# Half of the query transfers of a gated-attention kernel's first blocks issued from GpSimd and ScalarE

## The chip, the core and the metric

The kernel runs on one core of a Trainium2 chip. The metric is the time of one execution on the device in microseconds (us); the kernel before takes 1825.69 us, the median of three runs (1825.0 to 1826.87).

## What is computed

A linear attention whose state is a complex matrix that decays at each step, followed by a mixture of experts whose gates are balanced by eight rounds of normalizing rows and columns. Cut to what matters:

```python
# attention: B, H, S, D = 4, 8, 768, 48; a = a_re + i*a_im, scaled to magnitude <= 0.999
for t in range(S):
    S_ = a[t][:, None] * S_ + outer(k[t], v[t])      # S_ is complex, D x D for each head
    y[t] = q[t] @ real(S_)
x = y as [B*S, H*D]                                  # 3072 x 384
P = sinkhorn(exp(x @ w_gate), 8 rounds)              # 3072 x 8
out = sum over e of P[:, e] * (relu(x @ w1[e]) @ w2[e])
```

## The kernel before

**Blocks.** The 3072 positions are cut into 12 blocks of 256, three for each batch entry, and a block into two halves of 128 (`c` = 0, 1). Phase 1 goes through the blocks. For block i the elementwise part (`elem` and `chain`) normalizes the decays, forms their running products z (complex, two planes `a` = 0, 1 for real and imaginary) with a scan on VectorE (lines 304 to 309), and writes keys divided by the product into `kh` (line 416) and queries times the product back into `z` (line 418), channels on the partitions. Then `mix(i)` does the attention of the block in a chunked form, and two experts' layers for the block before it (`experts`, lines 164 to 193) are interleaved with it on TensorE: each step has a first layer `ph`, two evictions on ScalarE (`hh` line 191, `hf` line 192), a difference on VectorE (`hl`, line 193), and a second layer that runs three steps later (LAG = 3). Phases 2a and 2b do the remaining six experts and touch none of this.

**Transfers to head layout.** `mix` needs keys and queries with a head's channels on the partitions. For each half c it copies `kh` into `ks` and `z` into `qs` (lines 430 to 435): for each of the two tiles, both planes and three channel tiles, 12 transfers of 16 partitions by 8 heads by 128 positions (129 for `qs`; the last column is the state's decay over the half). A transfer is 64 KB, both sides in SBUF. The real plane goes to partitions 0 to 47, the imaginary one to 64 to 111. There are two buffers each of `qs` and `ks`, used by halves in turn.

**What follows.** TensorE transposes the keys (`keys`, line 454), multiplies keys by queries into scores (`scores`, line 468), and forms the state's update `U` (line 463). VectorE copies the scores under a causal mask into `sc` (line 471). `outs` (line 485) multiplies `sc` by the values and the old state by `qs`. VectorE then moves the state on (lines 511 to 522), and the output goes through ScalarE (`xh`, line 524) and VectorE (`xl`, line 525) to the experts.

**Order.** TensorE's instructions run in the order in which the program writes them. On the other engines and queues a scheduler orders them by program order and by its own estimate of when each is ready; each engine then works through its list in order, a transfer's issue among them: an issue that has to wait holds up what stands behind it. All transfers go through SP's queue, apart from two of the first `z`. In block 0 the instructions of `mix` on ScalarE and VectorE are told to stand behind the elementwise part, and the first weights are loaded in thirds (line 145) between its steps, behind the transfers on SP. `self.ql[i]` remembers a block's last transfer; the loads of `qk` (line 335) and `z` (line 333) of later blocks are told to stand behind it on SP. The blocks of `chain` that matter on ScalarE are the squares (lines 385, 391, 394, 405) and the reciprocal roots (lines 390, 410).

Of the kernel before, what the change touches and what calls it, by code (L numbers as in the profile page):

```python
# [20 lines left out]
NCH = SUB // CH  # L21
# [39 lines left out]
class Net:  # L61
# [134 lines left out]
    def phase1(self, c1, ca):  # L196
# [45 lines left out]
        for i in range(ns):  # L242
            mix = self.mix(i)
            if i == 0:
                n = 0
                while True:
                    with tc.issue_after(self.sqs[0, 1].ins), tc.issue_after(self.zl[0, 1].ins):
                        if next(mix, self) is self:
                            break
                    with tc.issue_after(self.sqs[0, 1].ins):  # L250
                        for _ in range(2 if n else 0):
                            if late and next(late[0], self) is self:
                                late.pop(0)
                                next(late[0], None) if late else None
                    n += 1
                for g in late:
                    for _ in g:
                        pass
                with tc.issue_after(self.gl.ins):
                    m = self.marks  # L260
                    self.behind = [m[j] for j in (0, 0, 0, 2, 2, 2, 3, 3, 3, 4, 5, 5)]
                    self.elem(1)
                edge = mybir.DependencyInfo(mybir.DependencyClass.NoSync, mybir.DependencyReason.DATA)
                for ins in self.casts:
                    tc.add_manual_dep(ins.ins, self.nrm.ins.name, edge, reason="casts behind the norm")
                continue
            lg = self.logits(i - 1)
            for n in range(2 * NF):
                with ExitStack() as st:
                    if i == 1 and n in (4, 5):  # L270
                        st.enter_context(tc.issue_after(self.sqs[1, n - 4].ins))
                        st.enter_context(tc.issue_after(self.zl[1, n - 4].ins))
                    self.moe.send((i - 1, n // NF, n % NF))
                if i == 1 and n == 2:
                    for ins in self.post[1]:
                        tc.add_manual_dep(ins.ins, self.hf.ins.name, edge, reason="chain behind the step")
                if n in (1, 2):
                    next(lg)
                if n >= LEAD.get(i, 4):
                    next(mix, None)  # L280
# [140 lines left out]
    def mix(self, i):  # L421
        nc, tmp = self.nc, self.tmp
# [5 lines left out]
        for c in range(NCH):  # L428
            ib = (i * NCH + c) % 2
            qs, ks, rr, rn = self.qs[ib], self.ks[ib], self.rr[ib], self.rn[ib]  # L430
            for dst, src, w in ((ks, kht, CH), (qs, zt, CH + 1)):
                for a in range(2):
                    for ct in range(NCT):
                        q = 64 * a + 16 * ct
                        dma = nc.sync.dma_start(dst[q:q + 16, :, :w], src[:, a, ct * NCH + c, :w])
            self.ql[i] = dma
            R = qs[:, :, CH]
            first = (i % self.nsub == 0) and c == 0
            lastc = (i % self.nsub == self.nsub - 1) and c == NCH - 1
# [576 lines left out]
```

## Time and profile before

| | us |
|---|---|
| median of the runs (lowest, highest) | 1825.69 (1825.0, 1826.87) |
| the profiled execution's own time | 1826.91 |
| its span, first to last instruction | 1825.0 |
| TensorE busy | 1767.9 |
| VectorE busy | 1358.4 |
| ScalarE busy | 733.1 |
| GpSimd busy | 6.4 |

Times in the rows are microseconds from the first instruction of the span, unless they say ns. PE is TensorE, PEld its weight loads, DVE VectorE, ACT ScalarE, POOL GpSimd, SP SyncE; a q behind a name (SPq, ACTq) is the engine's queue of instructions that issue transfers, wait or branch. L435 is line 435. `out<-in` are the program's names of what is written and read. In brackets at the end of a row stands how long the engine had been idle before it, and what ended that. PEclk is the share of TensorE's full clock that was granted: 1.00 is 2.4 GHz, 0.50 is 1.2 GHz.

### The profile page before, as it was taken

Reading aid. Unit: us, or ns where it says so; the run is one execution under the profiler, and the core shown is the slowest. Engines: PE = TensorE matmul, PEld = TensorE weight load, DVE = VectorE, ACT = ScalarE, POOL = GpSimd, SP = SyncE. Lnnn points to the kernel's source line nnn. Section 1 sums busy time; section 2 is a strip of 40 time slices with the busy share of each in tenths; the row PEclk is TensorE's granted clock in tenths of the full one; section 3 lists DMA queues with packets and bytes.
Section 4 is the critical chain, followed back from the end, with each engine's and each line's share of the span. In section 5 each row is a group of like instructions: output and inputs, shape, how many; then the busy total and the mean of one; then the engine's idle time right before and its main releaser. Section 6 shows DMA issues by size and latency. Waiting matters only on the chain.

```text
span 1825.0 us, 30537 instructions
## 1 busy us (share of the span) xinstructions
PE 1767.9 (97%) x12024; PEld 1726.8 (95%) x12024; DVE 1358.4 (74%) x3023; ACT 733.1 (40%) x1606; POOL 6.4 (0%) x15
## 2 busy tenths in 40 slices
PE   5899999999999999999999999999999999999998
PEld 3889899999999999899999999999999999999998
DVE  7898899889883587867576767687776767675754
ACT  7544444554543443434242424243433333342421
POOL 1000000000000000000000000000000000000000
PEclk9999999999999999999999999999999999999999
DMA  6334333433332431402020101232220101020100
GB/s 210 108 104 117 103 112 112 119 112 115 115 105 93 132 92 38 136 2 69 1 69 1 53 18 53 70 96 78 87 70 18 53 18 52 3 69 1 53 27 28
DMA packets 120632, 132.83 MB, mean 73 GB/s; under 512 B 9632, under 2 KB 100512, under 8 KB 120480
## 3 DMA queue, kind: packets, MB, share of 16 engines
q1 hardware_dynamic: 119680, 130.41, 23.3%
q8 instruction: 96, 1.57, 0.4%
q14 instruction: 56, 0.46, 0.1%
q10 hardware_dynamic: 800, 0.39, 0.1%
HBM read 88.22 MB, written 23.59 MB: 61 GB/s over the span
## 4 chain that ended last, share of the span: by engine, by line
PE 86%; DVE 8%; DMA 3%; ACT 1%; issue 1%; SPq 1%; DVEq 0%; ACTq 0%
PE po L741 10%; PE po L739 10%; PE po L740 10%; PE P L778 9%; PE P L780 9%; PE P L779 9%; PE po L164 4%; PE ph L186 3%; PE ph L187 3%; PE ph L185 3%; PE po L166 3%; PE po L165 3%; PE sp L468 3%; PE y L485 2%; PE U L463 1%
## 5 line engine op out<-in xcount | busy, mean ns | idle before, releaser
L741 PE MATMUL po<-wc,hl 128*128 128x384 f32 x1152 | 385.7, 335 | 2.9 <-DVE hl L800 2.9
L739 PE MATMUL po<-wc,hh 128*128 128x384 f32 x1152 | 385.2, 334 | 0.4 <-ACT hh L799 0.4
L740 PE MATMUL po<-wc,hh 128*128 128x384 f32 x1152 | 385.2, 334 | 0.0
L799 ACT ACTIVATE hh<-c 128x384 fp32r<-128x384 f32 x384 | 200.9, 524 | 322.1 <-DVE c L788 320.7
L800 DVE SCALAR_TENSOR_TENSOR hl<-c,hh 128x384 fp32r<-128x384 f32 x384 | 211.8, 552 | 65.8 <-ACT hh L799 58.0
L741 PEld LDWEIGHTS po<-wc,hl 128*128 128x128 f32 x1152 | 216.5, 188 | 4.4 <-DVE hl L800 4.4
L739 PEld LDWEIGHTS po<-wc,hh 128*128 128x128 f32 x1152 | 216.5, 188 | 0.7 <-ACT hh L799 0.7
L740 PEld LDWEIGHTS po<-wc,hh 128*128 128x128 f32 x1152 | 216.4, 188 | 0.0
L793 ACT ACTIVATE s<-P 128x384 f32<-128x384 f32 x192 | 94.1, 490 | 275.0 <-PE P L780 275.0
L191 ACT ACTIVATE hh<-ph 128x256 fp32r<-128x256 f32 x192 | 73.1, 381 | 249.4 <-PE ph L187 248.9
L186 PE MATMUL ph<-xl,w 128*128 128x256 f32 x576 | 162.9, 283 | 2.8 <-DVE xl L525 2.8
L185 PE MATMUL ph<-xh,w 128*128 128x256 f32 x576 | 162.2, 282 | 0.6 <-ACT xh L524 0.6
L187 PE MATMUL ph<-xh,w 128*128 128x256 f32 x576 | 162.5, 282 | 0.0
L778 PE MATMUL P<-B,wa 128*128 128x384 f32 x480 | 160.4, 334 | 0.6 <-DVE c L788 0.6
L780 PE MATMUL P<-B,wa 128*128 128x384 f32 x480 | 160.4, 334 | 0.0
L779 PE MATMUL P<-B,wa 128*128 128x384 f32 x480 | 160.3, 334 | 0.0
L164 PE MATMUL po<-w,hh 128*128 128x384 f32 x384 | 140.9, 367 | 1.1 <-ACT yst L169 1.1
L166 PE MATMUL po<-w,hl 128*128 128x384 f32 x384 | 130.1, 339 | 0.0
L165 PE MATMUL po<-w,hh 128*128 128x384 f32 x384 | 129.7, 338 | 0.0
L788 DVE TENSOR_TENSOR c<-P,u 128x384 f32<-128x384 f32 x192 | 106.2, 553 | 31.1 <-PE P L780 29.3
L788 DVE TENSOR_TENSOR u<-u,s 128x384 f32<-128x384 f32 x96 | 53.3, 555 | 100.9 <-ACT s L793 100.8
L193 DVE TENSOR_TENSOR hl<-hf,hh 128x256 fp32r<-128x256 f32 x192 | 80.0, 419 | 45.0 <-ACT hf L192 43.6
(172 smaller groups left out, 3649.3 us busy)
## 6 DMA issues: line engine op xcount, KB each, us to landing
raw<-in_w_dram SPq DMA_DIRECT2D x48, 768.0 KB, 4.3
qs<-z SPq DMA_DIRECT2D x144, 64.5 KB, 2.6
qk<-in_aqk_dram SPq DMA_DIRECT2D x12, 768.0 KB, 4.9
ks<-kh SPq DMA_DIRECT2D x144, 64.0 KB, 2.6
ye_d<-yst SPq DMA_DIRECT2D x48, 192.0 KB, 2.1
y<-ye_d SPq DMA_DIRECT2D x48, 192.0 KB, 2.4
z<-in_aqk_dram SPq DMA_DIRECT2D x11, 768.0 KB, 6.9
B<-x_d SPq DMA_DIRECT2D x40, 192.0 KB, 3.5
```

Source lines behind the costliest of these rows:

```text
L164: nc.tensor.matmul(po[k], hh[:, s], w2h, start=f == 0, stop=False)
L185: nc.tensor.matmul(ph, w[:, 0, cs], xh[:, ct, :], start=(ct == 0), stop=False)
L186: nc.tensor.matmul(ph, w[:, 0, cs], xl[:, ct, :], start=False, stop=False)
L187: nc.tensor.matmul(ph, w[:, 1, cs], xh[:, ct, :], start=False, stop=(ct == NCT - 1))
L739: nc.tensor.matmul(po[k], hh[:, s], w2[:, 0, i], start=first, stop=False)
L740: nc.tensor.matmul(po[k], hh[:, s], w2[:, 1, i], start=False, stop=False)
L741: nc.tensor.matmul(po[k], hl[:, s], w2[:, 0, i], start=False, stop=last)
L778: nc.tensor.matmul(ps, t[:, 0, k], x[:, 0], start=first, stop=False)
L779: nc.tensor.matmul(ps, t[:, 0, k], x[:, 1], start=False, stop=False)
L780: nc.tensor.matmul(ps, t[:, 1, k], x[:, 0], start=False, stop=last)
L799: A.activation(hh, c, AF.Relu)
L800: V.scalar_tensor_tensor(hl, c, 0.0, hh.bitcast(F32), ALU.max, ALU.subtract)
```

## The change

In blocks 0, 1 and 2 the three transfers of the queries' imaginary plane (a = 1) of each half are issued from another engine: from GpSimd in block 0, from ScalarE in blocks 1 and 2. That is 6 transfers on GpSimd and 12 on ScalarE that leave SP's queue. The transfers themselves, and blocks 3 to 11, stay as they are. `self.ql[i]` keeps the last transfer of the block that SP issues, so the loads that stand behind it stay on SP behind the real plane of the second half.

```diff
                 for a in range(2):
                     for ct in range(NCT):
                         q = 64 * a + 16 * ct
-                        dma = nc.sync.dma_start(dst[q:q + 16, :, :w], src[:, a, ct * NCH + c, :w])
-            self.ql[i] = dma
+                        second = dst is qs and a and i < 3
+                        dma = ((nc.scalar if i else nc.gpsimd) if second else nc.sync).dma_start(dst[q:q + 16, :, :w], src[:, a, ct * NCH + c, :w])
+                        self.ql[i] = self.ql.get(i) if second else dma
```

## Rows read from the trace of the kernel before

**Rows 1.** The page's busy times of the engines over the span.

```profile
PE 1767.9 (97%) x12024; PEld 1726.8 (95%) x12024; DVE 1358.4 (74%) x3023; ACT 733.1 (40%) x1606; POOL 6.4 (0%) x15
```

**Rows 2.** TensorE's waits over the span: us in total, times, longest.

```profile
PE sp L468 <- DMA qs<-z: 7.4, 3, 3.2
```

**Rows 3.** Windows: length, busy us of each engine, PEclk, DMA share, GB/s.

```profile
48.00:50.00 2.00, 2.00 (x13) 2.00 (x12) 1.91 (x5) 0.11 (x1) 0.00 (x0) 0.53 0.30 71
50.00:52.00 2.00, 2.00 (x21) 1.19 (x21) 1.93 (x6) 1.33 (x5) 0.00 (x0) 0.61 0.39 97
52.00:54.00 2.00, 2.00 (x17) 1.89 (x16) 1.06 (x3) 0.38 (x1) 0.00 (x0) 1.00 0.41 100
100.00:125.00 25.00, 22.50 (x256) 20.59 (x255) 24.25 (x71) 7.20 (x19) 0.00 (x0) 0.93 0.38 111
300.00:400.00 100.00, 100.00 (x933) 96.47 (x932) 88.96 (x205) 52.89 (x131) 0.00 (x0) 1.00 0.36 107
```

**Rows 4.** Timeline of SP's queue in block 0: start, length, what.

```profile
36.95 3.92 SPq L435 DMA_DIRECT2D ks<-kh  x6
40.98 3.76 SPq L435 DMA_DIRECT2D qs<-z  x6
...
54.11 1.76 SPq L145 DMA_DIRECT2D wr<-in_w_dram  x4
```

**Rows 5.** Timeline of VectorE in block 0.

```profile
38.25 0.55 DVE L418 TENSOR_TENSOR z<-z,qk 128x384 f32<-128x384 f32 x1
...
44.47 0.74 DVE L395 TENSOR_SCALAR x<-y 128x384 f32<-128x384 f32 x2
...
48.07 0.73 DVE L471 COPY_PREDICATED sc<-mask,sp 128x512 f32<-128x512 uint8 x1
...
53.02 0.73 DVE L471 COPY_PREDICATED sc<-mask,sp 128x512 f32<-128x512 uint8 x1 [0.94 <-PE sp L468]
...
59.08 0.56 DVE L525 TENSOR_TENSOR xl<-y,xh 128x384 fp32r<-128x384 f32 x1 [1.34 <-ACT xh L524]
...
66.70 0.73 DVE L471 COPY_PREDICATED sc<-mask,sp 128x512 f32<-128x512 uint8 x1 [1.09 <-PE sp L468]
```

**Rows 6.** Block 0: the last query transfer and output in the chain; the scores' timeline.

```profile
44.14 2.60 DMA qs<-z
...
50.95 0.88 PE y L485 x16
...
46.83 1.13 PE L468 MATMUL sp<-qs,ks 112*128 112x128 f32 x8 [2.94 <-DMA qs<-z]
```

**Rows 7.** Timelines of ScalarE, VectorE and TensorE in block 1.

```profile
88.29 0.38 ACT L191 ACTIVATE hh<-ph 128x256 fp32r<-128x256 f32 x1 [1.47 <-PE ph L187]
...
89.61 0.84 ACT L390 ACTIVATE y<-x 128x768 f32<-128x768 f32 x1 [0.66 <-DVE x L389]
...
92.01 0.96 DVE L392 TENSOR_TENSOR x<-x,zz 128x768 f32<-128x768 f32 x1 [0.40 <-ACT zz L391]
...
119.77 0.65 PE L485 MATMUL y<-sc,v 128*32 128x128 f32 x8 [2.42 <-DVE sc L471]
```

**Rows 8.** Timelines of VectorE, SP's queue and TensorE in block 2.

```profile
137.45 0.95 DVE L418 TENSOR_TENSOR z<-z,qk 128x768 f32<-128x768 f32 x1
...
138.89 5.12 SPq L435 DMA_DIRECT2D qs<-z  x6
...
138.89 1.91 SPq L435 DMA_DIRECT2D qs<-z  x1
...
146.36 0.91 PE L468 MATMUL sp<-qs,ks 112*128 112x128 f32 x6 [1.21 <-DMA qs<-z]
```

**Rows 9.** Timeline of TensorE in block 3.

```profile
191.26 1.83 PE L468 MATMUL sp<-qs,ks 112*128 112x128 f32 x8 [3.21 <-DMA qs<-z]
```

**Rows 10.** Tiles z and qs to 400 us: issue min/median/max in ns, landing; memset.

```profile
L343 ACTq DMA_DIRECT2D z<-in_aqk_dram x2: 443/448/453, 0.8 to 1.3; - x2
...
L435 SPq DMA_DIRECT2D qs<-z x96: 547/597/1979, 41.0 to 373.5; - x96
...
L213 POOL MEMSET qs<- x2: 949/949/949, 0.7 to 1.6; 32x1032 f32 x2
...
DMA to landing us min/median/max: 2.3/2.6/5.1
```

## The prediction

> **What bounds the kernel now.** I read the page's busy times first: TensorE is busy 1767.9 of 1825.0 us [rows 1], so all that a change of this size can give back lies in its gaps. Next the waits of TensorE. One of them touches the moved transfers: the score matmuls of line 468 waited for the landing of `qs` 7.4 us in three waits [rows 2]. The timeline of TensorE says where: 2.94 us at 46.83 (block 0, first half), 1.21 us at 146.36 (block 2, first half), 3.21 us at 191.26 (block 3) [rows 6, 8, 9]. Block 1 has none, and block 3 isn't changed. Last, the windows: from 300 to 400 us TensorE is busy for all of the 100 us [rows 3], so what it has gained by the end of block 3 should stay to the end.
>
> In block 0 the SP queue issues, one behind the other, six transfers of `ks` (from 36.95), six of `qs` (from 40.98), six and six of the second half, and only then four loads of weights at 54.11 [rows 4]. One issue takes 0.55 to 0.60 us and the data land 2.6 us after its start [rows 10]. The sixth `qs` starts at 44.14 and lands at 46.74; the scores start at 46.83 [rows 6]. After that wait the granted clock falls to the lower level, 1.2 GHz, for part of the next stretch: 0.53 from 48 to 50 us, 0.61 from 50 to 52, 1.00 again after that [rows 3].
>
> **The change part by part.** *Block 0, start of the scores.* The third `qs` on SP, now its last, is over two issues into the six: it starts at about 42.2 and lands at 44.8, so that the wait shrinks by three issues of 0.64 us, the spacing of the six in 3.76 us: 1.9 us. This holds if the three transfers on GpSimd are not later. They can begin when the imaginary half of the product with q is written, at 38.80 [rows 5]. No row shows a transfer that GpSimd issues. The lower bound is SP's 0.6 us each, the upper is that GpSimd gets nothing done while VectorE works without a pause (rival 3). I take 0.95 us, the only GpSimd instruction of the rows, a memset [rows 10]: the third starts at 40.7 and lands near 43.3, ahead of 44.8. Up to 1.7 us each, it stays hidden.
>
> *The clock.* The drop costs (1 - 0.53) x 2 + (1 - 0.61) x 2 = 1.7 us [rows 3]. The wait of 2.94 would shrink to 1.0; after a wait of 1.21 six score matmuls took 0.91 us, 0.15 each, while after 3.21 eight took 1.83, 0.23 each [rows 8, 9]. So I expect no drop there; bounds 0 and 1.7.
>
> *What is late next in block 0.* 1.9 and 1.7 are not both paid: the first mask copy on VectorE, 48.07 to 48.70, stands behind the normalizing of block 1 and can't come earlier [rows 5]. Before, the output matmuls that need it began at 50.95 [rows 6]; they would now begin about 48.8, and with the clock restored the stretch up to the second mask copy ends some 2.6 us earlier. VectorE follows, since it waited 0.94, 1.34 and 1.09 us there for TensorE and what hangs on it [rows 5], 3.4 in all. The weight loads at 54.11 follow too, six issues having left SP ahead of them. **Term 1: -2.6**, between -3.6 and 0 (below, rival 3 bounds the loss).
>
> *Block 1.* TensorE doesn't wait for `qs` here, so SP's shorter queue gains nothing. The six issues go to ScalarE's queue at 0.45 (its two issues at the start) to 0.60 us (SP's for this shape) [rows 10]; I take 0.60, the same shape, 3.6 us. Behind them stand the evictions `hh` and `hf`, which TensorE needs only some steps later, and line 390 of the next block's normalizing at 89.61. ScalarE's idle times before 88.29 and 89.61 are 1.47 and 0.66 [rows 7], so up to 1.5 us is left over and pushes line 390, line 391 and with them VectorE, which already waited 0.40 us for ScalarE at 92.01. VectorE is what TensorE waits for next, 2.42 us at 119.77 [rows 7]. Bounds 0 and +3.6; **term 2: +1.0**, since the first transfers can go ahead of 88.29.
>
> *Block 2.* The imaginary half is ready at 138.40, before SP's `qs` begin at 138.89; these six take until 144.01 because the first takes 1.9 us [rows 8]. With three on ScalarE, SP's last starts 1.9 us sooner, more than the 1.21 that TensorE waited at 146.36. ScalarE's part starts no later than its evictions let it. **Term 3: -1.2**, bounds -1.2 and 0. No normalizing waits on ScalarE in this stretch, and evictions a little late are covered by the three steps between `hl` and its use (LAG).
>
> *Block 3* is as before: its scores wait for SP's queue, and that for VectorE's keys. I cost it at nothing because VectorE and TensorE arrive there earlier by the same. If VectorE doesn't, the wait of 3.21 takes the gain back (rival 2). The loads of `qk` and `z` that stand behind the last `qs` on SP go out earlier, and an earlier load makes no reader later: nothing.
>
> Sum: -2.6 + 1.0 - 1.2 = -2.8 us. The profiled execution took 1826.91 us, its span 1825.0, so it would come to 1824.1; it lies 1.2 above the median of the runs, 1825.69, from which I forecast **1822.9 us**. A measurement of this kernel can tell about 0.2%, 3.65 us, from no change; the forecast is inside that.
>
> **Rivals.** *1, more comes back.* ScalarE's issues fit in its idle time (term 2 is 0), and the full 3.6 us of term 1 is paid or part of block 3's wait goes because a shorter SP queue meets fewer long issues like the 1.9 us one: -3.6 - 1.2 = -4.8, 1820.9 us. For it: ScalarE's idle rows of 1.47 and 0.66; against it: the mask copy at 48.07.
>
> *2, taken back.* ScalarE's six issues in block 1 push VectorE by the whole 1.5 to 3.6 us; TensorE then finds the mask copy at 119.77 and the queries at 191.26 as late as before, and its gains turn into longer waits there: about -0.3, 1825.4 us. For it: VectorE is busy for 24.25 of the 25 us from 100 to 125 [rows 3], so lateness stays. That the clock drop stays as well belongs here.
>
> *3, slower: GpSimd held off by VectorE.* Its place is 38.8 to 52 us, where VectorE's rows follow each other without a pause until the wait before 53.02 [rows 5]. If GpSimd can prepare its transfers only in that pause, they begin at 52.1, the third starts at 53.3 and lands at 55.9, 9 us behind the start of the scores before: 1825.7 + 9 - 0.2 = 1834.5 us. It decides from the point where the third lands later than 46.74. Against it: the rows of VectorE there are two-input forms, with one pair of the quick single-input form (line 395, 0.37 us each) [rows 5].
> The Trainium skill, "SBUF — State Buffer", section "SBUF: two separate sides", speaks against the change in this place: descriptors of GpSimd's transfers can't be written while VectorE runs in a two-port mode. Its section "A bandwidth-pool intuition that's wrong (but worth ruling out)" has 3.1 us for such a transfer that took 0.62 alone. By that figure three would land near 38.8 + 9.3 = 48.1, an estimate from that page, and the sum would be +1.1 in the place of -2.8. Its section "Who interferes with whom" gives `tensor_tensor` no such mode, which would leave the pair of line 395 alone to hold GpSimd off; no run shows it yet.
>
> *4, the change doesn't do what it says:* the transfers share engines with SP's, landing stretches from 2.6 us, and no score starts earlier. I put it with rival 2, as it also gives about 1825.5.
>
> **Chances.** Forecast 0.46, rival 1 0.26, rivals 2 and 4 0.18, rival 3 0.10. Faster by over 0.2% is under 1822.04: nearly all of rival 1 and a quarter of the forecast's own spread, 0.37. Slower by over 0.2% is rival 3, 0.10. The rest, 0.53, is within 0.2%. The range leaves out rival 3 and the far end of rival 1: 1819.5 to 1826.3. The forecast's own range is 1821.5 to 1824.5.
>
> **What would show it.** Right: three GpSimd issues from about 38.9 that land before 44.9; scores of block 0 near 44.9; clock 1.00 from 48 to 52; weight loads near 51; no wait for `qs` at block 2; waits near 117 and 188 that are about as long as before. Wrong: a GpSimd landing after 46.7; ScalarE line 390 over 1.5 us later behind line 390's own input; a wait at 117 longer by what block 0 gained.

## The result

The changed kernel takes 1835.62 us (median of 8 runs, 1834.27 to 1838.18) against 1826.33 for the kernel before, timed beside it: 9.3 us more, a ratio of 1.005 with a 95% interval of 1.004 to 1.0059. The prediction, 1822.9 us and at most 1826.3, was wrong in sign and in size. The profiled execution took 1835.58 us, its span 1833.6, which is 8.6 us longer than the span before.

**The profile after.** Behind line 435 every line stands one later than before: 454 is now 455, 468 is 469, 471 is 472, 485 is 486. First the page's busy times of the changed kernel, which answer to [rows 1]:

```profile
PE 1769.5 (97%) x12024; PEld 1728.6 (94%) x12024; DVE 1358.1 (74%) x3023; ACT 735.3 (40%) x1606; POOL 9.6 (1%) x21
```

TensorE's own work has hardly grown, 1.6 us, so most of the loss is waiting. The waits of TensorE from 30 to 260 us of the changed kernel, total, times and longest, answer to [rows 2]:

```profile
PE ktp L455 <- DMA ks<-kh: 9.1, 2, 6.9
...
PE sp L469 <- DMA qs<-z: 3.8, 2, 2.6
```

The scores do wait less for the queries, 3.8 us where it was 7.4. In their place the transposes of the keys wait 9.1 us for `ks`, a wait that the prediction did not name. TensorE's timeline of the changed kernel says where (start, length, what, idle time before and what ended it):

```profile
45.63 0.87 PE L455 MATMUL ktp<-ident,ks 112*128 112x112 f32 x4 [2.14 <-DMA ks<-kh]
47.78 2.05 PE L469 MATMUL sp<-qs,ks 112*128 112x128 f32 x8 [1.28 <-DMA qs<-z]
...
151.02 0.98 PE L455 MATMUL ktp<-ident,ks 112*128 112x112 f32 x4 [6.95 <-DMA ks<-kh]
154.56 1.83 PE L469 MATMUL sp<-qs,ks 112*128 112x128 f32 x7 [2.56 <-DMA qs<-z]
```

There are two places. In block 0 the scores start at 47.78 instead of 46.83 [rows 6]; 1.0 of this is a later start of everything, since TensorE's step at 37.93 before stands at 38.96 here. So nothing was gained there. (That 1.0 isn't the change's: the step stands ahead of the first moved transfer, and with block 0 alone moved, below, it starts at 38.11.) In block 2 TensorE stands still for 6.95 us ahead of the keys and 2.56 more ahead of the scores, where it waited 1.21 in all [rows 8].

**Why block 2's keys are late.** VectorE's and then ScalarE's timeline of the changed kernel in block 1, some 50 us earlier, answer to [rows 7]:

```profile
96.23 0.43 DVE L193 TENSOR_TENSOR hl<-hf,hh 128x256 fp32r<-128x256 f32 x1 [1.69 <-ACT hf L192]
98.94 0.75 DVE L472 COPY_PREDICATED sc<-mask,sp 128x512 f32<-128x512 uint8 x1 [2.29 <-PE sp L469]
...
99.90 0.95 DVE L392 TENSOR_TENSOR x<-x,zz 128x768 f32<-128x768 f32 x1
...
104.31 0.96 DVE L396 SCALAR_TENSOR_TENSOR x<-zz,x 128x768 f32<-128x768 f32 x1 [1.64 <-ACT zz L394]
```

```profile
96.08 0.50 ACT L169 ACTIVATE yst<-po 128x384 f32<-128x384 f32 x1
96.45 0.86 ACT L390 ACTIVATE y<-x 128x768 f32<-128x768 f32 x1
...
102.65 0.20 ACT L500 ACTIVATE rr<-qs 48x8 f32<-48x8 f32 x1
...
103.34 0.94 ACT L394 ACTIVATE zz<-y,bm 128x768 f32<-128x768 f32 x1
```

The reader is to see an order, not a duration. Before, VectorE did block 2's normalizing (lines 392 to 396) first and block 1's mask copy behind it. Now the mask copy stands ahead of line 392 and waits for TensorE's scores; VectorE is idle for 1.69 and 2.29 us. On ScalarE line 390 stands behind an output copy (line 169), and line 394 behind the three small copies of lines 500 to 502. Line 390 starts at 96.45 (before 89.61), line 392 at 99.90 (before 92.01) [rows 7]; 2.9 us of that stand already at line 389 (91.56, before 88.63). No row of ScalarE's own transfers is that long: its six issues end at 94.6. What moved is the list. The program's scheduler rewrote the lists of VectorE and ScalarE when the transfers moved: of VectorE's 3324 instructions 1008 stand at another place, of ScalarE's 1690 there are 333. TensorE's list is the same, instruction for instruction.

**Why block 0 gains nothing.** GpSimd's timeline of the changed kernel, and its transfers from 36 to 56 us (count, KB each, median us from issue to landing):

```profile
40.49 1.69 POOL L436 DMA_DIRECT2D qs<-z  x3 [33.53 <-DVE g L413]
```

```profile
ks<-kh SPq DMA_DIRECT2D x12, 64.0 KB, 4.2
qs<-z POOLq DMA_DIRECT2D x6, 64.5 KB, 4.3
qs<-z SPq DMA_DIRECT2D x6, 64.5 KB, 4.9
```

GpSimd isn't held off: three issues take 1.69 us. But transfers on both queues now take 4.2 to 4.9 us to land (medians over both halves), where SP's alone took 2.6 [rows 10]. The scores of the first half wait for SP's third query transfer; in the chain of the changed kernel it stands so (start, length):

```profile
43.24 4.41 DMA qs<-z
```

With the later start of 1.0 taken off, it is issued 1.9 us earlier than SP's sixth was before (44.14), as the prediction had it. But it lands after 4.41 instead of 2.60 us [rows 6], 1.8 us longer, and nothing is left.

Next, windows of the changed kernel and then of the kernel before (PEclk, DMA share and GB/s stand at the end). The first of each is a stretch in which the transfers of the block were moved without a pause, by both queues and by SP's alone:

```profile
40.00:50.00 10.00, 6.58 (x24) 4.71 (x22) 6.30 (x15) 6.85 (x20) 3.25 (x6) 0.67 1.03 122
...
46.00:56.00 10.00, 8.72 (x51) 7.46 (x50) 3.78 (x8) 5.44 (x16) 0.04 (x1) 0.50 0.86 91
```

```profile
38.00:48.00 10.00, 6.21 (x25) 4.23 (x26) 9.96 (x22) 8.32 (x22) 0.00 (x0) 0.83 0.40 99
...
46.00:56.00 10.00, 9.17 (x75) 7.97 (x79) 8.64 (x19) 4.52 (x15) 0.00 (x0) 0.83 0.41 103
```

A second queue moves more, 122 instead of 99 GB/s, but far less than two queues issue: while both issue, SP's one transfer of 64.5 KB per 0.63 us and GpSimd's one per 0.53 come to some 230 GB/s (an estimate from these issue times). What doesn't get through piles up as a later landing. (From 46 to 56 the changed kernel moves less, 91 instead of 103 GB/s, because little is left by 52: from 52 to 54 it moves 50.) The granted clock of TensorE is 0.50 from 46 to 56 us.

### The profile page after: what moved, and what is told of

The parts are those of the page before. It is cut to its first block, busy times and chain, and to the rows that moved or that the text cites. A ratio compares the mean times of both kernels' runs of the same rounds, so it can differ in the third digit from the quotient of the medians.

```text
span 1833.6 us, 30557 instructions
## 1 busy us (share of the span) xinstructions
PE 1769.5 (97%) x12024; PEld 1728.6 (94%) x12024; DVE 1358.1 (74%) x3023; ACT 735.3 (40%) x1606; POOL 9.6 (1%) x21
## 4 chain that ended last, share of the span: by engine, by line
PE 82%; DVE 11%; DMA 4%; issue 2%; ACT 1%; SPq 1%; DVEq 0%; ACTq 0%
PE po L742 10%; PE po L740 10%; PE po L741 10%; PE P L779 9%; PE P L781 9%; PE P L780 9%; PE po L164 3%; PE ph L186 3%; PE ph L187 3%; PE ph L185 3%; PE po L166 3%; PE po L165 3%; PE sp L469 2%; PE y L486 2%; DMA raw<-in_w_dram 2%
## 5 line engine op out<-in xcount | busy, mean ns | idle before, releaser
L186 PEld LDWEIGHTS ph<-xl,w 128*128 128x128 f32 x576 | 109.1, 189 | 4.9 <-DVE xl L526 4.8
## 6 DMA issues: line engine op xcount, KB each, us to landing
qs<-z SPq DMA_DIRECT2D x126, 64.5 KB, 2.7
```

Source lines behind the costliest of these rows:

```text
L186: nc.tensor.matmul(ph, w[:, 0, cs], xl[:, ct, :], start=False, stop=False)
```

## The experiments

All were timed in turn with the kernel before, whose median was 1826.87 us beside the first four runs below, 1826.56 beside three others (one stretch, block 0 from ScalarE, block 3 alone) and 1827.21 beside the rest. First each block alone; in the place of 0 stands 1 or 2 for the others.

```diff
-                        second = dst is qs and a and i < 3
+                        second = dst is qs and a and i == 0
```

**Block 0 alone.**

> Block 0's six transfers from GpSimd, blocks 1 and 2 as before. Landing theory (transfers of two queues at once slow each other, 4 to 6 us in the place of 2.6): the scores of block 0 start no earlier, 46 to 48 us, and the time is 1827 to 1829. Order theory (the scheduler's lists for VectorE and ScalarE cost the time): VectorE's list differs in block 0 only, so the mask copies wait there for 3 us each; also 1827 to 1829, but with VectorE's waits as the cause. ScalarE theory (issues in ScalarE's queue hold up its evictions): as before, 1826.

Measured 1829.2 us, ratio 1.0013 (1.0004 to 1.0022): 2.3 us lost where term 1 had gained 2.6. TensorE waits 2.03 us for the keys and 1.43 for the queries and begins the scores at 46.86, no earlier than before. The scheduler's list on VectorE differs in only 87 places. So the gain that term 1 counted isn't there. Where the 2.3 us arise, the trace doesn't show: one and the same step of TensorE behind block 3, of the kernel before and of this one, starts at the same time.

```profile
301.63 0.43 PE L485 MATMUL y<-sc,v 128*32 128x128 f32 x8
```

```profile
301.61 0.43 PE L486 MATMUL y<-sc,v 128*32 128x128 f32 x8
```

**Block 1 alone.**

> Block 1's six transfers from ScalarE alone. Order theory and ScalarE theory: line 390 of block 2's normalizing starts some 7 us later than before, the keys of block 2 are late by as much, and TensorE waits for them: 1831 to 1835, most of the 9 us. Landing theory: block 1's scores have time to spare, so 1826 to 1827.

Measured 1833.68 us, ratio 1.0033 (1.002 to 1.0046): 6.8 us, most of the whole loss, and the same wait in block 2. VectorE's list differs in 920 places. TensorE's timeline of this kernel:

```profile
147.66 0.98 PE L455 MATMUL ktp<-ident,ks 112*128 112x112 f32 x4 [6.76 <-DMA ks<-kh]
```

**Block 2 alone.**

> Block 2's six transfers from ScalarE alone. Landing theory: they land after 3.5 to 4.5 us and the scores of block 2 wait about as long as before or a microsecond longer, 1826 to 1827.5. Order theory: VectorE's list is nearly that of before, so 1826 and no more. ScalarE theory: its evictions are late by up to 2 us in block 2, 1827 to 1828. Prediction's term 3: 1.2 us less, 1825.

Measured 1825.88 us, ratio 0.9991 (0.9983 to 1.0). The wait for the queries is 0.45 us instead of 1.21, and the list on VectorE differs in 10 places. Term 3 has the right sign and about the right size.

These three don't say whether block 1 loses by ScalarE's six issues or by the new order, because both changed. So the next kernels hold one and change the other. The order is written out as dependencies between neighbours on one engine, which need no semaphore (cut here: the lists in `ORDER`, the lines that make `traced` and `edge`, and two lines of bookkeeping):

```diff
+        for e, seq in ORDER.items():
+            seq = [traced[n] for n in seq.split() if n in traced]
+            for p, t in zip(seq, seq[1:]):
+                tc.add_manual_dep(t, p.name, edge, reason="order written out")
```

**All 18 moved, the order of before.**

> All 18 transfers moved as in the change, but VectorE and ScalarE work through their lists in the order of the kernel before, written out (the issues on ScalarE go where the scheduler puts them). Order theory: the loss goes, 1824 to 1828. Landing theory: block 0 gains nothing and the loss stays by the late landings, 1829 to 1833. ScalarE theory: the issues still stand in its queue in blocks 1 and 2, 1831 to 1836.

Measured 1829.82 us, ratio 1.0016 (1.0008 to 1.0025). Of the 9.3 us, 6.3 are gone with the old order; what stays is 3.0. That is over the order theory's range and inside the landing theory's, but it can't be put down to the landings alone, since only the lists of VectorE and ScalarE were held here. SP's list changed with the rest: before, four loads of weights went out and then those of `qk` and `z` (54.11 to 56.83); here three loads of weights stand behind `qk` and `z`. Timelines of SP, ScalarE and TensorE of this kernel (line 481 reads the loaded weights):

```profile
52.35 0.34 SPq L480 DMA_DIRECT2D wr<-in_w_dram  x1
52.78 0.38 SPq L678 DMA_DIRECT2D qk<-in_aqk_dram  x1
54.20 0.38 SPq L676 DMA_DIRECT2D z<-in_aqk_dram  x1
56.14 2.19 SPq L480 DMA_DIRECT2D wr<-in_w_dram  x3
...
61.65 0.72 ACT L481 ACTIVATE w<-wr 128x256 fp32r<-128x256 f32 x2 [2.42 <-DMA wr<-in_w_dram]
...
63.43 0.98 PE L798 MATMUL ktp<-ident,ks 112*128 112x112 f32 x4 [2.91 <-issue]
```

With block 0 alone moved and the scheduler's own lists, three of the four loads stand ahead of `qk`, and TensorE comes to the same transposes at 60.10 without a wait. How much of the 3.0 us is SP's order, no run separates.

**Nothing moved, the order of the changed kernel.**

> All transfers on SP's queue as in the kernel before; only the order of the instructions on VectorE and ScalarE is that of the changed kernel. If most of the loss is the order (theory), this alone takes 1831 to 1834 us, with VectorE's mask copies ahead of the normalizing and the keys of block 2 some 7 to 10 us late at the transpose (a wait of TensorE near 148 of 5 us or more). If the loss needs the transfers on the other queues (rival), it takes 1826 to 1828 us.

Measured 1836.39 us, ratio 1.0044 (1.0031 to 1.0057), somewhat over the expected 1831 to 1834. All transfers are on SP here and the whole loss is there. TensorE's timeline of this kernel, where line 797 holds the transposes:

```profile
149.97 0.98 PE L797 MATMUL ktp<-ident,ks 112*128 112x112 f32 x4 [6.82 <-DMA ks<-kh]
153.96 2.04 PE L811 MATMUL sp<-qs,ks 112*128 112x128 f32 x8 [3.01 <-DMA qs<-z]
```

**Nothing moved, one stretch in the new order.** The lists of before, with VectorE's 198th to 308th instruction and ScalarE's of the same time as in the changed kernel.

> All transfers on SP's queue; VectorE's and ScalarE's order is that of the kernel before except for one stretch, 111 instructions on VectorE (the 198th to the 308th) and up to 62 on ScalarE from the same time, block 1's mask copies, evictions and normalizing, which stand in the order of the changed kernel. If that stretch makes most of the 9.5 us that the whole new order costs (theory), this takes 1831 to 1835 us, with the keys of block 2 some 5 to 7 us late at the transposes. If the loss is spread over the order of many blocks (rival), it takes 1826.5 to 1829.5 us and TensorE has no such wait near 148.

Measured 1835.92 us, ratio 1.0045 (1.0032 to 1.0059): 9.4 us from one stretch, a little more than the theory gave. Timelines of TensorE, VectorE and ScalarE of this kernel (line 797 transposes, 814 mask copy, 733 is line 390 of before, 739 is 396):

```profile
148.36 0.98 PE L797 MATMUL ktp<-ident,ks 112*128 112x112 f32 x4 [6.91 <-DMA ks<-kh]
...
96.32 0.75 DVE L814 COPY_PREDICATED sc<-mask,sp 128x512 f32<-128x512 uint8 x1 [2.29 <-PE sp L811]
...
101.68 0.96 DVE L739 SCALAR_TENSOR_TENSOR x<-zz,x 128x768 f32<-128x768 f32 x1 [1.65 <-ACT zz L737]
...
93.83 0.86 ACT L733 ACTIVATE y<-x 128x768 f32<-128x768 f32 x1
```

The same idle 2.29 us ahead of the mask copy, the same line 396 some 6.7 us late (95.02 before), and then SP's first issue of block 2's keys: 142.37 here, 135.02 before. VectorE has little slack in between (24.25 of 25 us busy before [rows 3]), so the lateness is carried over 40 us and comes out as TensorE's wait of 6.91. VectorE's keys and SP's first issue of them, before and then here:

```profile
134.04 1.82 DVE L416 TENSOR_TENSOR kh<-x,z 128x768 f32<-128x768 f32 x2
...
135.02 3.77 SPq L435 DMA_DIRECT2D ks<-kh  x6
```

```profile
141.38 1.82 DVE L759 TENSOR_TENSOR kh<-x,z 128x768 f32<-128x768 f32 x2
...
142.37 3.77 SPq L778 DMA_DIRECT2D ks<-kh  x6
```

The step of TensorE that stands at 301.63 before stands at 310.82 here: 9.2 of the 9.4 us are there by then. The new order gives something too, since TensorE's wait for the mask copy near 120 is 0.57 instead of 2.42 us [rows 7]; the 9.4 us are what is left. Whether VectorE's or ScalarE's part of the stretch would do it alone wasn't tried. Over the ten microseconds around that wait (146 to 156) the window shows a granted clock of 0.50, where the kernel before has 1.00; eight score matmuls take 2.05 us there (152.33) that took 1.13 before (146.36), so this is part of the 9.4 us as well:

```profile
146.00:156.00 10.00, 4.65 (x18) 4.36 (x19) 8.29 (x16) 0.54 (x1) 0.00 (x0) 0.50 0.41 102
```

```profile
146.00:156.00 10.00, 9.64 (x97) 9.34 (x98) 8.14 (x29) 3.13 (x10) 0.00 (x0) 1.00 0.49 127
```

**Block 1 moved, the order of before.**

```diff
-                        second = dst is qs and a and i < 3
+                        second = dst is qs and a and i == 1
```

> Block 1's six transfers alone are issued from ScalarE, and VectorE and ScalarE keep the order of the kernel before. If the order made block 1's loss of 6 to 7 us, this takes 1825.5 to 1827.5 us. If six issues of 0.6 us on ScalarE are enough to push the normalizing (rival), it takes 1831 us or more, with the normalizing of ScalarE 3 to 4 us later than 89.6.

Measured 1827.9 us, ratio 0.9995 (0.9987 to 1.0004): no difference (the median in microseconds lies 0.4 over the expected upper end; the ratio, taken beside its own runs of before, says the same). ScalarE's and TensorE's timelines of this kernel:

```profile
88.87 1.76 ACTq L779 DMA_DIRECT2D qs<-z  x2
90.68 0.85 ACT L733 ACTIVATE y<-x 128x768 f32<-128x768 f32 x1 [2.12 <-DMA qs<-z]
...
119.98 0.43 PE L829 MATMUL y<-sc,v 128*32 128x128 f32 x8 [2.42 <-DVE sc L815]
```

The issues do push line 390, from 89.61 to 90.68, by 1.1 us, as the prediction had it. TensorE's wait near 120 stays 2.42 us [rows 7], so the push costs nothing that can be measured. The rival, that six issues on ScalarE make the loss, falls. Writing out an order costs nothing that shows either.

Now block 0's loss. **From ScalarE instead of GpSimd, old order.**

```diff
+                        second = dst is qs and a and i == 0
+                        dma = (nc.scalar if second else nc.sync).dma_start(dst[q:q + 16, :, :w], src[:, a, ct * NCH + c, :w])
```

> Block 0's six transfers alone, issued from ScalarE in the place of GpSimd, in the order of instructions of the kernel before. If the path is shared, whatever queue issues (theory), the transfers on both queues land in 3.5 us or more where they overlap, the scores of block 0 start no earlier than before (46.5 to 48), and the time is 1826.5 to 1830 us. If it is GpSimd's queue that lands slowly (rival), they land in 2.6 us, the scores start at 44.5 to 45.5, and the time is 1822.5 to 1825 us.

Measured 1830.84 us, ratio 1.0019 (1.001 to 1.0028), a little over the theory's range. Transfers of this kernel from 36 to 56 us, and TensorE's timeline:

```profile
ks<-kh SPq DMA_DIRECT2D x12, 64.0 KB, 3.6
...
qs<-z ACTq DMA_DIRECT2D x6, 64.5 KB, 3.5
qs<-z SPq DMA_DIRECT2D x6, 64.5 KB, 4.0
```

```profile
47.05 1.13 PE L812 MATMUL sp<-qs,ks 112*128 112x128 f32 x8 [1.05 <-DMA qs<-z]
```

Another queue, stretching on both again, and no earlier scores. It isn't GpSimd that lands slowly. (SP's list has three loads of weights behind `qk` and `z` here too, so the 4.3 us aren't the price of the landings alone.)

**GpSimd's transfers behind the keys, old order.**

```diff
+                        if second:
+                            tc_.add_manual_dep(dma.ins, key.ins.name, mybir.DependencyInfo(mybir.DependencyClass.Sync, mybir.DependencyReason.DATA), reason="queries behind the keys")
+                        if dst is ks:
+                            key = dma
```

> Block 0's six transfers alone are issued from GpSimd, in the order of instructions of the kernel before, and each half's three wait for that half's last transfer of keys to land. If it is the shared path that makes block 0 slower (theory), the keys land in 2.6 us again, TensorE waits under 1 us ahead of the key transposes, the scores of block 0 start at 46.8 to 47.8, and the time is 1825 to 1828 us. If a transfer from GpSimd is slow in itself (rival), it lands 4 us or more after its issue even with less beside it, the scores start at 48.5 or later, and the time is 1829 us or more.

Measured 1835.01 us, ratio 1.0034 (1.0022 to 1.0046): worse, and here the expectation fell, not only its numbers. The first half's keys land in 2.5 to 2.7 us again and TensorE doesn't wait for them, as foreseen. But the queries now come behind them, and SP's second-half keys beside the queries. GpSimd's and TensorE's timelines of this kernel:

```profile
42.73 1.72 POOL L779 DMA_DIRECT2D qs<-z  x3 [35.77 <-DVE z L761]
49.95 1.57 POOL L779 DMA_DIRECT2D qs<-z  x3 [5.51 <-DMA ks<-kh]
```

```profile
47.96 1.41 PE L817 MATMUL sp<-qs,ks 112*128 112x128 f32 x5 [4.85 <-DMA qs<-z]
```

By its time this run fits the rival, but its first GpSimd transfer, issued at 42.73 with little beside it, lands as fast as SP's do (KB, us to landing):

```profile
qs<-z POOLq DMA_DIRECT2D x1, 64.5 KB, 2.7
```

So a transfer from GpSimd isn't slow in itself, and the rival falls. The wait that orders the transfers has moved the delay from the keys to the queries. TensorE waits a further 3.50 us at 64.73, at the transposes that waited 2.91 with all 18 moved: ScalarE waited 3.01 us until 63.26 for a load of weights, and SP had issued the load of `qk` at 48.03, ahead of all four.

**Looking for a gain: blocks 2 and 3 from ScalarE, and block 3 alone (i == 3), old order.**

```diff
-                        second = dst is qs and a and i < 3
+                        second = dst is qs and a and i in (2, 3)
```

> The transfers of the imaginary half of blocks 2 and 3 are issued from ScalarE, all others from SP, and VectorE and ScalarE keep the order of the kernel before. By the theory (late issues cost only where TensorE waits for the queries, and only the order and the shared path cost anything) block 2's wait of 1.2 us and part of block 3's 3.2 us go: 1823 to 1825.5 us. If the shared path takes back what the shorter queue gives (rival), the keys land later by as much and the time is 1826 to 1828 us.

Measured 1823.73 us, ratio 0.9984 (0.9974 to 0.9994), the one kernel of this study that beats both, by 0.16%. Its profiled execution, 1828.31 us, is the slowest of its twelve, and the step at 301.63 before stands at 301.44 in it, so the trace can't show where the 0.16% come from. Block 2's wait of 1.21 us is gone. Block 3's is split in TensorE's timeline:

```profile
188.85 0.60 PE L798 MATMUL ktp<-ident,ks 112*128 112x112 f32 x4 [1.30 <-DMA ks<-kh]
191.10 2.04 PE L812 MATMUL sp<-qs,ks 112*128 112x128 f32 x8 [1.64 <-DMA qs<-z]
```

> The transfers of the imaginary half of block 3 alone are issued from ScalarE, in the order of instructions of the kernel before. With block 2's as well the time was 0.16% under the kernel before. If block 2's wait was the source of that gain, this takes 1826 to 1827.5 us and the wait of 3.2 us in block 3 stays in the keys' transposes or the scores; if block 3's wait was, it takes 1823 to 1825.5 us and the waits near 190 together are 2.5 us or less.

Measured 1824.87 us, ratio 0.9992 (0.9983 to 1.0001), which doesn't tell it from no change. The waits in block 3 are 1.58 for the keys and 1.56 for the queries, together 3.14 against 3.21 [rows 9]: what the queries gained, the keys lost. In the time expected by one case and the waits by the other, this run is inconclusive; the two gains, block 2's and block 3's, aren't separated beyond what block 2 alone (0.9991) shows.

## Why the prediction was wrong, point by point

**Term 2 (block 1, +1.0, bounds 0 and +3.6) is the step that failed most.** Its mechanism, six issues pushing line 390, is there with 1.1 us and costs nothing that shows. But the term took the order of all other instructions as given, though the part on order ahead of it says that a scheduler makes the lists. Moving six issues to ScalarE changed its estimate, it put a mask copy ahead of the normalizing, and the new order of one stretch on VectorE and ScalarE alone is 9.4 us with every transfer still on SP. Why the scheduler chose so was only argued, from when it would think ScalarE's results ready; no run shows its estimates. The sum of the prediction had no term for it, and no rival either: rival 3 was on the slower side with 1834.5 us, near the measured time, but its mechanism, GpSimd held off by VectorE, is not there (0.53 to 0.64 us per issue). That its number lies near is chance.

**Term 1 (block 0, -2.6) had the wrong sign; block 0 alone costs 2.3.** The step that failed is the landing of 2.6 us taken for transfers on two queues at once. Rival 4 had this mechanism, at no cost. The 1.9 us of earlier issue on SP were eaten by a landing that took 1.8 us longer (4.41). That explains why nothing was gained; why 2.3 us are lost stays open, since TensorE isn't late by 301.61 us in that kernel's trace, and the landings, the 87 places of VectorE's list and SP's changed list weren't separated. The clock, for which the term had a gain of up to 1.7 us, went the other way: 0.50 from 46 to 56 us, and 0.54 with block 0 alone, against 0.83 before. That clock is not settled as the cause, since executions with block 0 untouched show 0.66 (block 1 moved, old order) and 0.51 (block 2 alone) for that stretch at a time that isn't longer. Of the signs that the prediction named for right, a clock of 1.00 from 48 to 52 and weight loads near 51 (the first starts at 52.94) failed here at once.

**Term 3 (block 2, -1.2) held** where it could be seen alone: 1.0 us by the medians, 0.09% by the ratio with an interval that reaches no change, and a wait of 0.45 us where none was expected. In the changed kernel it couldn't show, because block 2's keys came 10 us late.

**Together.** By the medians, the new order alone costs 9.2 us, the moved transfers with the old order on VectorE and ScalarE 3.0, both 9.3. The two don't add. SP's list isn't the same in these kernels, so why they don't isn't shown; that the transfers' delays fall into time that TensorE waits anyway is a guess.

**The sentence from the Trainium skill**, "SBUF — State Buffer", section "A bandwidth-pool intuition that's wrong (but worth ruling out)", would have had GpSimd's three transfers land near 48.1 by 3.1 us each, an estimate from that page. The result of +1.1 for the sum was nearer to the truth in sign, but not by its mechanism: the issues took 0.53 to 0.64 us here beside a busy VectorE, and the same stretching came with ScalarE's queue.

## What to carry to other kernels

Where a scheduler orders the lists, a change of one queue changes the order on others: compare the lists before and after, and cost the re-ordering as a term of its own. If the gain of a change is wanted, hold the order fixed and time both; here the 18 moved transfers cost 9.3 us with the new lists and 3.0 with the old ones of VectorE and ScalarE, and those of blocks 2 and 3 gained 0.16% with the old. Hold every list, those of the transfer queues too: SP's was left free here and put loads in another order. A second queue pays only where the path can take what both issue: look at whether GB/s grows as the issues do, and at the landing times.

## What was not expected of the hardware

For transfers of 16 partitions within SBUF, SP's queue alone moved 99 GB/s at a DMA share of 0.40, which reads like a path in use for two fifths. A second queue brought it to 122 GB/s, a quarter more, at a share of 1.03. The landing of a 64 KB transfer stretched from 2.6 to between 3.5 and 4.9 us (medians), whether the second queue was GpSimd's or ScalarE's. A share well under 1 is thus no sign of that much room. Nor is it a share of busy time that ends at 1, as a window of the changed kernel shows (1.28):

```profile
50.00:52.00 2.00, 2.00 (x12) 2.00 (x12) 2.00 (x5) 0.54 (x2) 0.00 (x0) 0.50 1.28 110
```

What in the path is the limit, no run here shows.
